# Chunked attention into a softplus feed-forward layer: other queues for the ring loads, spills and weight sums, other bank pairs in the products, another start of the second m-tile

## The chip, the cores and the metric

The kernel runs on one core of a Trainium2 chip. The metric is the device time of one execution in microseconds (us); before the change it is 883.77 us, the median of three runs (883.25 to 886.02). The engines are TensorE (PE, with its weight loads PEld), VectorE (DVE), ScalarE (ACT), GpSimd (POOL) and SyncE (SP); transfers between DRAM and on-chip memory are issued by SP, ACT or POOL and run on 16 DMA engines. Each engine works through its own instructions in program order.

## The reference

Eight batches, eight heads, 576 positions of 64 values: attention within chunks of 64 positions, then a feed-forward layer with softplus over all 4608 tokens. All in fp32.

```python
def _attn_ref(q, k, v):
    q_c = q.reshape(B, H, nc, chunk, D)          # nc = 9 chunks of 64, k_c and v_c alike
    scores = scale * np.matmul(q_c, k_c.transpose(0, 1, 2, 4, 3))
    scores = scores - np.max(scores, axis=-1, keepdims=True)
    attn = np.exp(scores)
    attn = attn / (np.sum(attn, axis=-1, keepdims=True) + 1e-09)
    return np.matmul(attn, v_c).reshape(B, H, S, D)

def _moe_ref(x, w_in, w_out):                    # x: 4608 x 512, w_in: 512 x 2048, w_out: 2048 x 512
    h = x @ w_in
    g = np.maximum(h, 0.0) + np.log1p(np.exp(-np.abs(h)))
    return g @ w_out
```

## The kernel before

**Numbers.** Each fp32 matmul is made of three faster ones: both factors are split into a rounded high part and the rest (names ending in hi and lo), and hi·hi, lo·hi and hi·lo are summed in PSUM. PE thus runs three matmuls of 128x512 for one, and ACT (the copies that round: `g_hi`, L643) and DVE (the subtractions: `g_lo`, L647) work ahead of it.

**Tiles.** The 4608 tokens are 9 m-tiles of 512, d_ff is 16 f-chunks of 128. For an m-tile and an f-chunk the first matmul gives 128 x 512 of h in a PSUM tile `pa`, softplus gives u, u is split into `g_hi` and `g_lo`, and the second matmul (L818, twelve matmuls, called G2 or a step here) adds to four tiles `po` that stand through all 16 f-chunks and are then copied out (L825) and stored (L832).

**Two stages.** The first three m-tiles are done plainly (L631 first matmul, L639 softplus). The last six form three *supers* of two m-tiles and eight *pairs* of f-chunks. In a pair a Strassen scheme takes seven products P0 to P6 (L763, six matmuls each) for eight: a product needs sums of two weight blocks and sums of two x blocks. The four quarters of the result lie in four PSUM banks x, y, z, v, two in each of two `pa` tiles a and b; P4, P5 and P6 add to y, z and x. ACT copies three banks out as s0, s1, s2 (L769), DVE and POOL make the six mixes d, e, c22, f, f2, c11 (L782), and ACT takes softplus of the quarters, soft10 and soft01 from y and z, soft11 from c22, soft00 from c11 (L790). Dependences in PSUM go by whole `pa` tiles, so a write to one bank waits for reads of its neighbour. The quarters of the first m-tile (soft10, soft00) go on to their G2s at once, two per pair behind the products of the next pair. Those of the second m-tile (soft01, soft11) are spilled to DRAM (L795) and come back (L798) for a phase of 16 G2s after the eight pairs.

**Ring.** The weight sums are made once, in the plain stage: POOL adds (L680, L694) and subtracts (L702), ACT rounds (L698), six stores per pair put them into a DRAM scratch (L708), and twelve more the weights that are needed unsummed (L714). Each pair of each super then reads its seven blocks in two transfers (L720, L724, "ring loads"): the large one has what P0 to P3 need, the small one P4 to P6.

**Attention.** Chunks of q, k, v are loaded by SP (L477, L358), transposed on DVE (L484, L531), scored on PE (L507), and P·V runs on PE (L595). For later m-tiles this happens in *bursts* of two blocks, put between the steps of the plain stage and into the first two supers, three among the pairs and one later. The exp of a burst needs another table of ACT than softplus; each change is a table load of 1.28 us.

**What sets the order.** Nothing is in the order of the code. `Plan` (L34 to L146) takes tasks with an engine, a cost, needs, an urgency `urg` (the lower first) and pools of buffers, simulates all engines with these costs and emits the instructions in the order of the simulated starts. PE's order is a list of its own; for the others the urgencies decide among what is ready. DMAs of SP and ACT share eight completion semaphores (DMAHW0 to 7), and a DMA waits for the one eight before it; the planner counted them by engine (`landed`). GpSimd's DMAs have others (DMASW).

Of the kernel before, what the change touches and what calls it, by code (L numbers as in the profile page):

```python
# [33 lines left out]
class Plan:  # L34
# [8 lines left out]
    WARM_UNTIL = 90.0  # L43

# [13 lines left out]
    def order(self):  # L58
# [37 lines left out]
        while times:  # L96
# [3 lines left out]
            for eng in list(wait):  # L100
# [5 lines left out]
                t = min(can, key=lambda t: (t["urg"], t["seq"]))  # L106
                wait[eng].remove(t)
# [10 lines left out]
                if t["kb"]:  # L118
                    end, lanes = now, landed.setdefault(eng, [0.0] * self.FLYING)
# [30 lines left out]
def chunked_attention_softplus_ffn(  # L150
# [84 lines left out]
    top_all = const.tile([P, TOP_BUFS * UW], I32, name="top")  # L235
    nc.vector.memset(top_all, 0)
    tops = [top_all[:, j * UW : (j + 1) * UW] for j in range(TOP_BUFS)]
    low_all = const.tile([P, LOW_BUFS * UW], I32, name="low")
# [415 lines left out]
    NX = 4  # L654

# [13 lines left out]
    def w_image(w, k):  # L669
        if w["name"] == "0_0" and k < NX:  # L670
            return raw_tile(1 + k // 2).bitcast(F32R)[:, k % 2 * MT : (k % 2 + 1) * MT]
        t = x_of(FAST - 1)[k // NX].rearrange("p s k t -> p (s k t)")
        return t[:, k % NX * MT : (k % NX + 1) * MT]

# [7 lines left out]
    def w_sum_parts(j):  # L682
        wt = live["wt", j]
        s, h = top_all.bitcast(F32), low_all.bitcast(F32)
        return [(s[:, :MT], h[:, :MT]), (s[:, MT:], h[:, MT:]), (wt[:, HC : 2 * HC], wt[:, :HC])]

    def w_sums(j, n):
        (s0, _), (s1, _), (s2, _) = w_sum_parts(j)
        t = [live["wt", j][:, i * HC : (i + 1) * HC] for i in range(4)]
        out, a, b, op = (  # L690
            (s0[:, :HC], t[0], t[3], ALU.add), (s0[:, HC:], t[2], t[3], ALU.add), (s1[:, :HC], t[2], t[0], ALU.subtract),
            (s1[:, HC:], t[0], t[1], ALU.add), (s2, t[1], t[3], ALU.subtract),
        )[n]
        nc.gpsimd.tensor_tensor(out, a, b, op=op)  # L694

    def w_sum_hi(j, n):
        s, h = w_sum_parts(j)[n]
        nc.scalar.copy(h.bitcast(F32R), s)  # L698

    def w_sum_lo(j, n):  # L700
        s, h = w_sum_parts(j)[n]
        nc.gpsimd.tensor_tensor(s, s, h, op=ALU.subtract)  # L702

    def w_sum_store(j, n, q):
        to = scratch[j].rearrange("p (n q c) -> p n q c", n=7, q=2)
        at = (slice(0, 2), slice(3, 6, 2), slice(6, 7))[n]
        src = w_sum_parts(j)[n][1 - q]
        nc.scalar.dma_start(to[:, at, q], src.rearrange("p (n c) -> p n c", c=HC))  # L708

    def w_own_store(b, q, i):  # L710
        src = wi[b][q].bitcast(F32)[:, i::2, 2 * i : 2 * i + 2, :].rearrange("p a k f -> p a (k f)")
        to = scratch[(0, 4, 6)[b] : (4, 6, 8)[b]]
        to = to.rearrange("a p (n q c) -> p a n q c", n=7, q=2)[:, :, 2 + 2 * i, q]
        nc.scalar.dma_start(to, src)  # L714

    def ring_load(w, part):
        src = scratch[w["j"]]
        if w["name"] == "0_0" and part == 0:
            for n in range(2):
                nc.scalar.dma_start(raw_tile(1 + n, True), src[:, 2 * n * MT : 2 * (n + 1) * MT])  # L720
# [3 lines left out]
        nc.scalar.dma_start(t[:, : cols.stop - cols.start], src[:, cols])  # L724
# [46 lines left out]
    def mix(w, what):  # L771
# [4 lines left out]
            "e": (s1, s1, s2, ALU.add),  # L776
            "c22": (s1, s1, v, ALU.add),
# [10 lines left out]
    def soft(w, i, j):  # L788
        src = {(0, 0): tmp_of(3), (0, 1): w["bank"][2], (1, 0): w["bank"][1], (1, 1): tmp_of(0)}[i, j]
        nc.scalar.activation(u_tiles(j)[i], src, AF.Softplus)  # L790
        if j == 0:
            w["first"][i]["u"] = u_tiles(0)[i]

    def spill_store(w):
        nc.scalar.dma_start(spill[w["s"]][w["j"]], top_all.bitcast(F32))  # L795

    def spill_load(w):
        nc.scalar.dma_start((top_all, low_all)[w["j"] % 2].bitcast(F32), spill[w["s"]][w["j"]])  # L798
        for i in range(2):
            w["second"][i]["u"] = u_tiles(1 - w["j"] % 2)[i]  # L800
# [3 lines left out]
    def gemm2(w):  # L804
# [9 lines left out]
        for n, (j, t) in order:  # L814
            if w["g"] == NG - 1 and t == TPM - 1:
# [4 lines left out]
                start=(w["first"] and n == 0), stop=n == 2 and (w["last"] or w["g"] == NG - 2 and t == TPM - 1),  # L820
# [55 lines left out]
    HOME_FREE.update({("v", i): ["Tq13", "Tk13"] for i in (12, 13)})  # L876
# [437 lines left out]
```

## Time and profile before

| stretch, us | what runs | length | PE busy | mean granted clock of PE |
|---|---|---|---|---|
| 89.0 to 336.7 | plain m-tiles, bursts, weight sums | 247.7 | 232.1 | 0.97 |
| 336.7 to 475.0 | super 1, pairs | 138.3 | 132.0 | 1.00 |
| 475.0 to 520.6 | super 1, second m-tile | 45.6 | 42.8 | 0.96 |
| 520.6 to 660.0 | super 2, pairs | 139.4 | 133.3 | 1.00 |
| 660.0 to 704.6 | super 2, second m-tile | 44.6 | 41.4 | 1.00 |
| 704.6 to 830.0 | super 3, pairs | 125.4 | 122.9 | 1.00 |
| 830.0 to 882.2 | super 3, second m-tile, end | 52.2 | 48.5 | 1.00 |

The profiled execution took 884.0 us by itself, with a span of 882.2 us from its first instruction to its last; 1.8 us lie around it. The three timed runs took 883.77, 886.02 and 883.25 us. A busy PE is not PE at its peak, since a matmul's shown end overlaps the next one; the loss is read from start to start. Waits are named by what released them, so "PE pa L763 <- DVE wib L782" is a product that waited for a mix.

### The profile page before, as it was taken

Reading aid. Unit: us, or ns where it says so; the run is one execution under the profiler, and the core shown is the slowest. Engines: PE = TensorE matmul, PEld = TensorE weight load, DVE = VectorE, ACT = ScalarE, POOL = GpSimd, SP = SyncE. Lnnn points to the kernel's source line nnn. Section 1 sums busy time; section 2 is a strip of 40 time slices with the busy share of each in tenths; the row PEclk is TensorE's granted clock in tenths of the full one; section 3 lists DMA queues with packets and bytes.
Section 4 is the critical chain, followed back from the end, with each engine's and each line's share of the span. In section 5 each row is a group of like instructions: output and inputs, shape, how many; then the busy total and the mean of one; then the engine's idle time right before and its main releaser. Section 6 shows DMA issues by size and latency. Waiting matters only on the chain.

```text
span 882.2 us, 15154 instructions
## 1 busy us (share of the span) xinstructions
PE 834.6 (95%) x5745; PEld 676.0 (77%) x5745; DVE 521.4 (59%) x876; ACT 388.8 (44%) x614; POOL 242.0 (27%) x217
## 2 busy tenths in 40 slices
PE   8899998999978999999998999999999999999998
PEld 7688887778756887777876877877777777878886
DVE  4999865656655588465566587473756733222322
ACT  4857753543423565343433254333452543333322
POOL 1676763359534221211110031121110312121100
PEclk9999999999989999999999999999999999999999
DMA  9987747664644535867567536757573145445332
GB/s 225 234 199 204 216 112 220 172 165 107 169 90 110 112 85 158 226 173 189 154 184 209 139 78 200 206 153 209 160 208 133 48 155 178 146 155 167 124 107 79
DMA packets 226343, 140.20 MB, mean 159 GB/s; under 512 B 183776, under 2 KB 207328, under 8 KB 223328
## 3 DMA queue, kind: packets, MB, share of 16 engines
q10 hardware_dynamic: 29408, 84.03, 28.9%
q1 hardware_dynamic: 196864, 55.23, 28.5%
q8 instruction: 45, 0.74, 0.4%
q14 instruction: 26, 0.21, 0.1%
HBM read 101.71 MB, written 36.70 MB: 157 GB/s over the span
## 4 chain that ended last, share of the span: by engine, by line
PE 66%; DVE 11%; DMA 8%; ACT 4%; issue 4%; POOL 3%; SPq 3%; ACTq 0%; DVEq 0%; POOLq 0%
PE po L818 36%; PE pa L763 20%; PE pa L631 7%; DVE wib L782 2%; DVE g_lo L647 2%; DVE eT L531 2%; SPq L477 2%; DMA raw<-in_moe_w_out_dram 2%; PE pa L595 1%; DMA q<-in_q_dram 1%; ACT low L790 1%; SPq L349 1%; PE pa L507 1%; DMA raw<-in_moe_w_in_dram 1%; POOL wib L782 1%
## 5 line engine op out<-in xcount | busy, mean ns | idle before, releaser
L818 PE MATMUL po<-late,g_hi 128*128 128x512 f32 x539 | 168.0, 395 | 0.1
L782 POOL TENSOR_TENSOR wib<-wib 128x512 f32<-128x512 f32 x48 | 62.6, 1304 | 333.3 <-ACT wib L769 331.4
L763 PE MATMUL pa<-wib,xb 128*128 128x512 f32 x432 | 109.0, 397 | 13.5 <-DVE wib L782 9.4
L818 PE MATMUL po<-wo_hi,g_lo 128*128 128x512 f32 x288 | 111.7, 400 | 9.6 <-DVE g_lo L647 9.6
L818 PEld LDWEIGHTS po<-late,g_hi 128*128 128x128 f32 x539 | 101.1, 189 | 22.0 <-POOL late L322 0.6
L818 PE MATMUL po<-wo_hi,g_hi 128*128 128x512 f32 x288 | 111.7, 400 | 2.5 <-ACT g_hi L643 2.5
L818 PE MATMUL po<-late,g_lo 128*128 128x512 f32 x287 | 109.1, 394 | 4.4 <-DVE g_lo L647 4.4
L763 PE MATMUL pa<-wi_hi,xb 128*128 128x512 f32 x368 | 113.3, 389 | 0.0
L818 PE MATMUL po<-wo_lo,g_hi 128*128 128x512 f32 x288 | 110.8, 397 | 0.6 <-POOL wo_lo L322 0.6
L763 PEld LDWEIGHTS pa<-wib,xb 128*128 128x128 f32 x432 | 79.2, 188 | 39.3 <-DVE wib L782 19.2
L531 DVE STREAM_TRANSPOSE eT<-qe 32x256 f32<-32x256 f32 x232 | 100.5, 433 | 8.2 <-POOL qe L582 4.9
L647 DVE TENSOR_TENSOR g_lo<-low,g_hi 128x512 fp32r<-128x512 f32 x72 | 54.4, 757 | 73.1 <-ACT g_hi L643 72.6
L643 ACT CAST g_hi<-low 128x512 fp32r<-128x512 f32 x72 | 44.7, 621 | 87.8 <-PE po L818 84.9
L763 PEld LDWEIGHTS pa<-wi_hi,xb 128*128 128x128 f32 x368 | 69.1, 188 | 14.3
L769 ACT COPY wib<-pa 128x512 f32<-128x512 f32 x72 | 40.0, 590 | 82.1 <-PE pa L763 82.1
L818 PEld LDWEIGHTS po<-wo_hi,g_lo 128*128 128x128 f32 x288 | 55.2, 192 | 24.9 <-DVE g_lo L647 13.4
L639 ACT ACTIVATE u<-pa 128x512 f32<-128x512 f32 (+1 forms) x50 | 29.1, 581 | 97.8 <-PE pa L631 52.7
L763 PE MATMUL pa<-wi_lo,xb 128*128 128x512 f32 x184 | 71.6, 389 | 0.0
L818 PEld LDWEIGHTS po<-late,g_lo 128*128 128x128 f32 x287 | 54.3, 189 | 18.0 <-DVE g_lo L647 6.6
L818 PEld LDWEIGHTS po<-wo_hi,g_hi 128*128 128x128 f32 x288 | 54.8, 192 | 14.7 <-ACT g_hi L643 3.2
L782 DVE TENSOR_TENSOR wib<-wib,pa 128x512 f32<-128x512 f32 x72 | 49.1, 687 | 27.9 <-ACT top L790 14.7
L818 PEld LDWEIGHTS po<-wo_lo,g_hi 128*128 128x128 f32 x288 | 55.1, 192 | 12.7 <-POOL wo_lo L322 1.1
(181 smaller groups left out, 1281.1 us busy)
## 6 DMA issues: line engine op xcount, KB each, us to landing
xb<-scratch ACTq DMA_DIRECT2D x23, 1024.0 KB, 5.4
xb<-scratch ACTq DMA_DIRECT2D x24, 768.0 KB, 5.1
spill<-top ACTq DMA_DIRECT2D x24, 512.0 KB, 3.3
out_dram<-raw SPq DMA_DIRECT2D x35, 256.0 KB, 2.9
raw<-in_moe_w_in_dram SPq DMA_DIRECT2D x16, 512.0 KB, 5.9
raw<-in_moe_w_out_dram SPq DMA_DIRECT2D x16, 512.0 KB, 4.9
raw<-in_v_dram SPq DMA_DIRECT2D x96, 64.0 KB, 2.9
top<-spill ACTq DMA_DIRECT2D x12, 512.0 KB, 4.0
```

What stands on the lines that cost most here:

```text
L349: eng.dma_start(dst[p0 : p0 + rows], src[b, :, s0 : s0 + rows, :].rearrange("h s d -> s h d"))
L477: nc.sync.dma_start(dst[p : p + BL, :, tb, :], src[b, :, s0 : s0 + BL, dh * BL : (dh + 1) * BL].rearrange("h s d -> s h d"),)
L507: nc.tensor.matmul(pa[o, c2, col : col + C], qT[r, a * HP + hl, :], kT[r, a * HP + hl, :], start=True, stop=True,)
L531: nc.vector.transpose(live["eT", i][d : d + BL, tb], e[s : s + BL, kb])
L631: nc.tensor.matmul(ph, wt[:, c, :], x[:, ts_, c, :], start=(n == 0), stop=(n == 3 * KC - 1))
L639: nc.scalar.activation(w["u"], w["ph"], AF.Softplus)
L643: nc.scalar.copy(w["hi"], w["u"])
L647: (nc.gpsimd if pool else nc.vector).tensor_tensor(w["lo"], w["u"], w["hi"].bitcast(F32), op=ALU.subtract)
L763: nc.tensor.matmul(w["bank"][BANK[k]], wts[:, q, c, :], x[:, c, :], start=k < NX and c + n == 0, stop=c == 1 and n == 2, skip_group_check= ...
L769: nc.scalar.copy(tmp_of(n), w["bank"][n])
L782: (nc.gpsimd if what in MIX_POOL else nc.vector).tensor_tensor(out, a, b, op=op)
L818: nc.tensor.matmul(pos[w["m"]][t], terms[n][0][:, j * P : (j + 1) * P], terms[n][1], start=(w["first"] and n == 0), stop=n == 2 and (w["la ...
```

## The change

- **Queues.** Ring loads are issued by GpSimd, spills, spill loads, weight-sum stores and own stores by SP; ACT issues none of them any more. `top` and `low` become two halves of one tile `ends`, and the sums are laid out hi beside lo, so that three stores per pair (512, 512, 256 KB) do for six. The blocks lie in the scratch in the order of `PLACE`.
- **Banks.** Tile a has x and v, tile b has y and z (before: x and y, z and v). P4 waits for s1 and s2, P6 for s0 and e; e takes s1 + v on DVE and c22 adds s2 on POOL; f and soft10 come behind P5.
- **Second m-tile.** The last pair's soft01 and soft11 are not spilled; their two G2s begin the second phase, and seven spills and loads per super remain.
- **Order.** An engine other than PE holds a task of `urg` 0 or more back when one of `urg` under 0 becomes ready within 0.7 us (from 120 us on). SP's and ACT's DMAs are counted together. Both exps of a burst get urgency −6, the fourth burst stands behind f-chunk 4 of the second phase, its seventh G2, and no longer behind f-chunk 8, its ninth, q and k of some blocks load into `raw` tiles, and some evacuations wait for transposes. PE's row count stays the same.

```diff
+    HOLD = 0.7
+    HOLD_FROM = 120.0
                 t = min(can, key=lambda t: (t["urg"], t["seq"]))
+                if t["urg"] >= 0 and now > self.HOLD_FROM and eng != "PE" and any(
+                    w["urg"] < 0 and now < ready[w["name"]] <= now + self.HOLD for w in wait[eng]
+                ):
+                    continue
-                    end, lanes = now, landed.setdefault(eng, [0.0] * self.FLYING)
+                    end, lanes = now, landed.setdefault(eng == "POOL", [0.0] * self.FLYING)
...
+    PLACE = (1, 2, 0, 3, 6, 4, 5)
+    def on(what):
+        return {"ACT": nc.scalar, "SP": nc.sync, "POOL": nc.gpsimd}[QUEUE[what]]
-    def w_sum_store(j, n, q):
-        to = scratch[j].rearrange("p (n q c) -> p n q c", n=7, q=2)
-        at = (slice(0, 2), slice(3, 6, 2), slice(6, 7))[n]
-        src = w_sum_parts(j)[n][1 - q]
-        nc.scalar.dma_start(to[:, at, q], src.rearrange("p (n c) -> p n c", c=HC))
+    def w_sum_store(j, n):
+        to = scratch[j][:, (1 + 2 * n) * MT :]
+        src = live["wt", j][:, :MT] if n == 2 else ends.bitcast(F32)[:, 2 * n * MT : 2 * (n + 1) * MT]
+        on("wd").dma_start(to[:, : src.shape[1]], src)
-        nc.scalar.dma_start(t[:, : cols.stop - cols.start], src[:, cols])
+        on("ring").dma_start(t[:, : cols.stop - cols.start], src[:, cols])
...
-            w["bank"] = [t[:, n] for t in (pa_tile(), pa_tile()) for n in range(2)]
+            a, b = pa_tile(), pa_tile()
+            w["bank"] = [a[:, 0], b[:, 0], b[:, 1], a[:, 1]]
-            "e": (s1, s1, s2, ALU.add),
-            "c22": (s1, s1, v, ALU.add),
+            "e": (s1, s1, v, ALU.add),
+            "c22": (s1, s1, s2, ALU.add),
-        nc.scalar.dma_start(spill[w["s"]][w["j"]], top_all.bitcast(F32))
+        on("us").dma_start(spill[w["s"]][w["j"]], top_all.bitcast(F32))
-        nc.scalar.dma_start((top_all, low_all)[w["j"] % 2].bitcast(F32), spill[w["s"]][w["j"]])
+        on("ul").dma_start((low_all, top_all)[w["j"] % 2].bitcast(F32), spill[w["s"]][w["j"]])
...
+    IN_RAW = {11: FAST - 1, 12: None, 13: None, 14: FAST, 15: FAST + 1, 16: None, 17: None}
+    HOMES.update({(n, 2 * p + 1): ("raw", 2 + j) for p in IN_RAW for j, n in enumerate("qk")})
-    IN_SUPER = ((0, 2), (0, 5), (0, 7), (1, 8))
+    IN_SUPER = ((0, 2), (0, 5), (0, 7), (1, 4))
-    MIX_POOL = ("d", "e")
+    MIX_POOL = ("d", "c22")
-    W_URG = 30
+    W_URG = 40
+    QUEUE = dict(wd="SP", wo="SP", ring="POOL", us="SP", ul="SP")
+    ISSUE = dict(ACT=0.4, SP=0.57, POOL=1.0)
-        second = [v_ for w in mine for v_ in w["second"]]
+        second = [v_ for w in mine[-1:] + mine[:-1] for v_ in w["second"]]
-            plan.add(f"exp{i}", "ACT", 0.62, partial(att_exp, i), [f"sub{b}"], urg=d, table="exp",
+            plan.add(f"exp{i}", "ACT", 0.62, partial(att_exp, i), [f"sub{b}"], urg=d if key in BEGIN else -6, table="exp",
-            needs += [before[f"P{k}_{name}"]] + {4: [f"s1_{name}"], 5: [f"s2_{name}"], 6: [f"s0_{name}"]}.get(k, [])
+            needs += [before[f"P{k}_{name}"]] + {4: [f"s1_{name}", f"s2_{name}"], 6: [f"s0_{name}", f"e_{name}"]}.get(k, [])
-                take = [("pa", [f"c11_{name}", f"soft10_{name}"]), ("pa", [f"soft01_{name}", f"c22_{name}", f"f2_{name}"])]
+                take = [("pa", [f"c11_{name}", f"e_{name}"]), ("pa", [f"soft01_{name}", f"soft10_{name}", f"f2_{name}"])]
-            ("d", ["s1", "s2"]), ("e", ["s0", "d"]), ("c22", ["e", "P3"]), ("f", ["d", "P4"]), ("f2", ["f", "P5"]),
+            ("d", ["s1", "s2"]), ("e", ["s0", "P3"]), ("c22", ["e", "d"]), ("f", ["d", "P5"]), ("f2", ["f", "P5"]),
-        for i, jj, what in ((1, 0, "P4"), (0, 1, "P5"), (1, 1, "c22"), (0, 0, "c11")):
+        for i, jj, what in ((1, 0, "P5"), (0, 1, "P5"), (1, 1, "c22"), (0, 0, "c11")):
-        plan.add(f"us{name}", "ACT", 0.6, partial(spill_store, w), [f"soft01_{name}", f"soft11_{name}"], urg=-1, kb=330)
+        if j < FC // 2 - 1:
+            plan.add(f"us{name}", QUEUE["us"], ISSUE[QUEUE["us"]], partial(spill_store, w), [f"soft01_{name}", f"soft11_{name}"], urg=-1, kb=400)
```

What it moves is seen in the order of three places, which the planner decides.

*A steady pair of the third super.* ACT before; `wib<-pa` are the copies s0 to s2, `low` and `top` the softplus quarters, "waits" the semaphores a row waits for:

```order
L769 COPY wib<-pa 128x512 [waits PE_49]
L769 COPY wib<-pa 128x512 [waits Pool_49]
L769 COPY wib<-pa 128x512 [waits PE_49]
L724 DMA xb<-scratch 128x2048 [waits DMAHW3_49]
L790 ACTIVATE low<-pa 128x512 [waits DVE_49,PE_49]
L790 ACTIVATE top<-pa 128x512 [waits DMAHW4_49,DVE_49]
L790 ACTIVATE top<-wib 128x512
L795 DMA spill_111<-top 128x1024 [waits Activation_49]
L724 DMA xb<-scratch 128x1536 [waits DMAHW5_49,PE_49]
L790 ACTIVATE low<-wib 128x512 [waits DVE_49]
L643 CAST g_hi<-low 128x512 [waits PE_49]
L643 CAST g_hi<-low 128x512 [waits PE_49,Activation_49]
```

and now:

```order
L779 COPY wib<-pa 128x512 [waits PE_49] x2
L779 COPY wib<-pa 128x512
L800 ACTIVATE ends<-pa 128x512 [waits DVE_49,PE_49]
L800 ACTIVATE ends<-pa 128x512 [waits DMAHW1_49,DVE_49]
L800 ACTIVATE ends<-wib 128x512 [waits Pool_49]
L800 ACTIVATE ends<-wib 128x512 [waits DVE_49,Activation_49]
L649 CAST g_hi<-ends 128x512 [waits PE_49,Activation_49] x2
```

The three DMA rows are gone, and the third copy, s2, has no wait of its own, since P2 is already awaited by s1. POOL at the change from the second super to the third, before (`wib<-wib` are d and the second POOL mix, `wib<-xa` sums of x blocks):

```order
L702 TENSOR_TENSOR raw_1379<-raw_1379 128x256
L742 TENSOR_TENSOR low<-xa 128x1024
L742 TENSOR_TENSOR top<-xa 128x1024
L782 TENSOR_TENSOR wib<-wib 128x512 x16
L742 TENSOR_TENSOR wib<-xa 128x1024 x2
```

and now:

```order
L733 DMA xb<-scratch 128x2048
L733 DMA xb<-scratch 128x1536
L751 TENSOR_TENSOR wib<-xa 128x1024 x2
L792 TENSOR_TENSOR wib<-wib 128x512 x2
L733 DMA xb<-scratch 128x2048
```

Before, the sixteen mixes of a super stood one behind the other; now both ring loads of the next pair stand between each two.

*The plain stage, a burst.* DVE before, around the wait of PE at 284.66 us (`qe<-xa` and `ka<-xa` are transposes of loaded q and k, `eT` of exponentials):

```order
L531 STREAM_TRANSPOSE eT<-qe 32x256 x4
L484 STREAM_TRANSPOSE qe<-q 128x512
L484 STREAM_TRANSPOSE ka<-k 128x512
L484 STREAM_TRANSPOSE qe<-xa 128x512
L484 STREAM_TRANSPOSE ka<-xa 128x512
L647 TENSOR_TENSOR g_lo<-u,g_hi 128x512 x2
```

and now:

```order
L537 STREAM_TRANSPOSE eT<-qe 32x256 x4
L490 STREAM_TRANSPOSE qe<-q 128x512
L490 STREAM_TRANSPOSE ka<-k 128x512
L653 TENSOR_TENSOR g_lo<-u,g_hi 128x512
L490 STREAM_TRANSPOSE qe<-xa 128x512
L653 TENSOR_TENSOR g_lo<-u,g_hi 128x512
L490 STREAM_TRANSPOSE ka<-xa 128x512
```

Both g_lo have moved ahead of a transpose. In the burst before 146.82 us one g_lo moved likewise, from behind `qe<-xb` to between two groups of four `eT`.

*Into the second m-tile.* ACT at the end of the third super's pairs, before (`low<-spill` and `top<-spill` load spilled quarters, `raw<-po` copies the first m-tile's result out):

```order
L790 ACTIVATE low<-wib 128x512 [waits DVE_49]
L643 CAST g_hi<-low 128x512 [waits PE_49]
L798 DMA top<-spill_111 128x1024 [waits DMAHW4_49]
L643 CAST g_hi<-low 128x512 [waits PE_49,Activation_49]
L798 DMA low<-spill_111 128x1024 [waits DVE_49]
L643 CAST g_hi<-top 128x512 [waits DMAHW5_49,PE_49]
```

and now:

```order
L800 ACTIVATE ends<-wib 128x512 [waits DVE_49,Activation_49]
L649 CAST g_hi<-ends 128x512 [waits PE_49,Activation_49] x2
L649 CAST g_hi<-ends 128x512 [waits DVE_49,PE_49]
L834 COPY raw_7738<-po_7121 128x512 [waits PE_49]
L834 COPY raw_7744<-po_7123 128x512 [waits DMAHW7_49,DMAHW0_49,PE_49]
```

The third `g_hi`, the first of the second m-tile, waited for a DMA and now waits for PE and DVE alone.

More of the change, by code (lines that the diff above doesn't have):

```diff
@@ L819, in gemm2 @@
                 pos[w["m"]][t], terms[n][0][:, j * P : (j + 1) * P], terms[n][1],
-                start=(w["first"] and n == 0), stop=n == 2 and (w["last"] or w["g"] == NG - 2 and t == TPM - 1),
+                start=(w["first"] and n == 0), stop=n == 2 and (w["last"] or w["g"] == END[0] and t == TPM - 1),
             )
@@ L1267, in add_g2 @@
                     continue
-                plan.add(f"ev{m}_{t}", "DVE" if odd else "ACT", 0.65, partial(evacuate, w, t), [f"G2_{g}"], urg=-3,
+                past = {FAST: 13, FAST + 1: 14, FAST + 2: 17}.get(m)
+                past = [f"T{n}{2 * past + 1}" for n in "qk"] if past and t < 2 else []
+                plan.add(f"ev{m}_{t}", "DVE" if odd else "ACT", 0.65, partial(evacuate, w, t), [f"G2_{g}"] + past, urg=-3,
                          take=[(f"out{t}", [f"st{m}_{t}"])] if m < NM - 1 else [],
```

93 lines of the change are left out of this document (49 added, 44 removed).

## Prediction

> **What bounds the kernel now.** The first view read is the page: the span and the busy time of each engine.
>
> ```profile
> span 882.2 us, 15154 instructions
> PE 834.6 (95%) x5745; PEld 676.0 (77%) x5745; DVE 521.4 (59%) x876; ACT 388.8 (44%) x614; POOL 242.0 (27%) x217
> ```
>
> PE is busy for 95% and the change leaves its matmuls as they are, so the only time to win is what PE loses between them. What a matmul costs with nothing lost is read in the timeline, from the first and the twelfth start of one undisturbed step of the second matmul:
>
> ```profile
> 275.30 0.39 PE L818 MATMUL po<-wo_hi,g_hi 128*128 128x512 f32 x1
> 277.79 0.39 PE L818 MATMUL po<-wo_hi,g_lo 128*128 128x512 f32 x1
> ```
>
> That is 2.49/11 = 0.226 us from start to start. A product of six therefore takes 1.36 us, a step of twelve 2.72 us; whatever starts later than this is loss, also where no idle time is printed, because busy times of neighbours overlap. The third view is the waits of PE, for the stage of plain m-tiles (90 to 336 us) and then for the supers (336 us to the end): releaser, total us, count, mean.
>
> ```profile
> PE po L818 <- DVE g_lo L647: 9.2, 5, 3.3
> PE pa L595 <- ACT u L639: 3.3, 2, 2.1
> PE pa L507 <- DVE ka L484: 2.9, 2, 2.0
> ```
>
> ```profile
> PE pa L763 <- DVE wib L782: 9.4, 8, 1.6
> PE po L818 <- DVE g_lo L647: 4.8, 5, 2.0
> PE pa L763 <- ACT low L790: 2.7, 4, 0.7
> PE po L818 <- ACT g_hi L643: 2.5, 1, 2.5
> ```
>
> Some waits cost more than themselves: the granted clock drops behind them. In the table of windows (length; busy us of PE, PEld, DVE, ACT, POOL; then PE's clock, DMA share, GB/s) four stretches stand out:
>
> ```profile
> 216.00:232.00 16.00, 13.89 (x172) 11.20 (x171) 7.36 (x14) 6.46 (x11) 11.14 (x12) 0.89 0.58 142
> 248.00:262.00 14.00, 9.91 (x149) 7.84 (x148) 8.26 (x15) 4.72 (x7) 7.00 (x9) 0.76 0.40 75
> 275.00:290.00 15.00, 11.69 (x45) 9.17 (x44) 4.90 (x8) 2.97 (x5) 7.34 (x8) 0.89 0.46 90
> 470.00:482.00 12.00, 9.14 (x33) 6.78 (x32) 7.24 (x16) 5.37 (x8) 0.00 (x0) 0.86 0.77 204
> ```
>
> Window times (1 − clock) gives 1.8, 3.4, 1.6 and 1.7 us. The Trainium skill, "TensorE: Matmul & The Clock Gate", section "Part 1: The HAM clock gate", puts the fall to half clock after an idle window of about 3.4 us. The trace differs in the last window, where the longest wait is 2.54 us (row 476.12 below); by the page its 1.7 us would not be there to win, and the measurement decides.
>
> **The change part by part.** *The pairs (24).* Each runs seven products; the waits stand at P4 to P6. A pair with an attention burst beside it, where ACT also loads tables, and a steady one, in the timeline:
>
> ```profile
> 388.12 2.88 PE L763 MATMUL pa<-wib,xb 128*128 128x512 f32 x12
> 392.46 1.66 PE L763 MATMUL pa<-wib,xb 128*128 128x512 f32 x6 [1.46 <-DVE wib L782]
> 393.96 0.39 PE L818 MATMUL po<-wo_hi,g_hi 128*128 128x512 f32 x1
> ...
> 726.93 4.68 PE L763 MATMUL pa<-wib,xb 128*128 128x512 f32 x18
> 731.45 0.39 PE L818 MATMUL po<-wo_hi,g_hi 128*128 128x512 f32 x1
> ```
>
> The first loses 393.96 − 388.12 − 18 × 0.226 = 1.76 us, of which 1.46 is printed, so refilling the pipe costs 0.30; the second loses 0.44 with nothing printed. The group of these matmuls has the idle time of all pairs:
>
> ```profile
> L763 PE MATMUL pa<-wib,xb 128*128 128x512 f32 x432 | 109.0, 397 | 13.5 <-DVE wib L782 9.4 <-ACT low L790 2.7
> ```
>
> 13.5 + 24 × 0.30 = 20.7 us lost in all. What P4 to P6 wait for follows from the whole-tile dependence: before, P6 (tile a) comes behind soft10 and f, which read P4's bank of the same tile. These are the steady pair's other engines, apart:
>
> ```profile
> 724.41 1.08 ACT L769 COPY wib<-pa 128x512 f32<-128x512 f32 x2 [2.27 <-PE pa L763]
> 728.49 0.60 ACT L790 ACTIVATE low<-pa 128x512 f32<-128x512 f32 x1 [0.77 <-PE pa L763]
> 729.19 0.69 DVE L782 TENSOR_TENSOR wib<-pa,wib 128x512 f32<-128x512 f32 x1 [6.21 <-ACT low L790]
> 727.80 2.65 POOL L782 TENSOR_TENSOR wib<-wib 128x512 f32<-128x512 f32 x2 [13.31 <-ACT wib L769]
> ```
>
> With the new banks P4 and P5 share tile b and P6 goes to tile a, whose last reader is e, one DVE operation of 0.69 us behind P3. P6 starts two products, 2.72 us, after P3's end: 2.0 us of room. soft10 and f (728.49, 729.19) no longer stand ahead of P6. What is late next is P4, which now waits for both s1 and s2: two ACT copies, 1.08 us, which begin when P2 ends and end about 1.3 us into P3 (1.08 and some 0.2 of latency), where P4 is due at 1.36. That is even, so I leave 0.2 us a pair, 4.8; nothing left and the steady pair's 0.44 are the bounds. **−16 us** (−21 to −10). It hangs on ACT being free then; moving the ring and spill issues off ACT (some 0.33 us each, as in row 471.43 below) helps there.
>
> *Ring loads on GpSimd.* 47 transfers; from ACT they land as follows (page part 6; below it min/median/max of all):
>
> ```profile
> xb<-scratch ACTq DMA_DIRECT2D x23, 1024.0 KB, 5.4
> xb<-scratch ACTq DMA_DIRECT2D x24, 768.0 KB, 5.1
> ```
>
> ```profile
> DMA to landing us min/median/max: 4.9/5.3/7.9
> ```
>
> The large one can go when P3 has read its tile, but stands on POOL behind d and c22 (2.65 us, row 727.80), which start 1.4 us into P3: issued 4.1 us after P3's start. The next P0 comes after P3 to P6 (5.4) and two steps (5.4): 10.9. Room 6.8 against 5.4: **0 us**, hidden under two second-matmul steps; more where a burst lies between. A GpSimd issue is not in the trace. Its landing is bounded by 4.9 and 7.9, nothing to 23 × 1.1 = +25 us; I take the median, 5.3, the same bytes on the same 16 engines. Time that the issue keeps POOL, 0 to 1.3 us (one mix), twice a pair, falls into POOL's 13.3 idle us. The small load waits on POOL for P6; behind it stand only the next pair's d and c22, which need later products anyway.
>
> *Spills and weight sums on SP.* ACT no longer issues 47 ring loads, 48 spill transfers, 48 sum stores and 12 own stores; SP issues 42, 24 and 12 of the last three kinds. ACT is no bound at 44%, so by itself **0**. A spill store now stands on SP behind loads that may wait for a buffer, and the next pair's soft01 waits for the store; it has most of a pair, 15 us by the steps above, and a ring load of twice its size landed in 5.4, so it is hidden. In the plain stage a store that waits for POOL's sums now holds the q and k loads behind it, and for those wait transposes and scores; SP already stands still there (waits of SP's queue, 100 to 345 us):
>
> ```profile
> SPq L477 <- DMA scratch<-low: 16.0, 7, 6.8
> ```
>
> That row also says that SP and ACT share DMA lanes: loads waited for scratch stores. Half the stores take half of it away, the order brings it back; the sum is in the plain stage's bounds below.
>
> *Into the second m-tile (3 times).* Before, its first softplus tile must come back from DRAM:
>
> ```profile
> 471.43 0.33 ACTq L798 DMA_DIRECT2D top<-spill  x1
> 475.45 1.14 ACT L643 CAST g_hi<-top 128x512 fp32r<-128x512 f32 x2
> 476.12 0.50 PE L818 MATMUL po<-wo_hi,g_hi 128*128 128x512 f32 x1 [2.54 <-ACT g_hi L643]
> 477.25 0.80 PE L818 MATMUL po<-wo_hi,g_lo 128*128 128x512 f32 x1 [0.32 <-DVE g_lo L647]
> ```
>
> With the last pair kept on chip g_hi needs only softplus, and the first reload has two steps, 5.4 us, for the 4.0 that 471.43 to 475.45 shows. That frees 2.54 + 0.32, two refills that I put at 0.2 each here, and the clock's 1.7: 5.0, of which I count 4.5. The other g_lo waits of the supers, 4.8 − 0.3 + 4 × 0.2 = 5.3, are at these transitions and beside the moved fourth burst; I count half, 2.6. **−7 us** (−10 to −2).
>
> *The plain stage.* Printed 9.2 + 3.3 + 2.9 = 15.4, nine refills of 0.17 and the clock's 6.8 make about 24 us to win. Two waits in it have one cause, a g_lo placed on DVE behind transposes that wait for loads:
>
> ```profile
> 279.42 0.71 DVE L484 STREAM_TRANSPOSE qe<-xa 128x512 f32<-128x512 f32 x1 [2.52 <-DMA xa<-in_k_dram]
> 282.98 0.71 DVE L484 STREAM_TRANSPOSE ka<-xa 128x512 f32<-128x512 f32 x1 [2.84 <-DMA xa<-in_k_dram]
> 283.61 1.00 DVE L647 TENSOR_TENSOR g_lo<-u,g_hi 128x512 fp32r<-128x512 f32 x1
> ```
>
> ```profile
> 146.82 0.50 PE L818 MATMUL po<-wo_hi,g_lo 128*128 128x512 f32 x1 [2.76 <-DVE g_lo L647]
> 284.66 0.50 PE L818 MATMUL po<-wo_hi,g_lo 128*128 128x512 f32 x1 [3.31 <-DVE g_lo L647]
> ```
>
> The plan's hold, costs and urgencies show only as order, and the new order has these two g_lo ahead of those transposes: 2.76 + 3.31 + 1.6 of clock, 7.7 us. The rest (P·V behind a softplus that splits two exps, scores behind late transposes) is helped by the paired exps and hurt by SP's stores. **−8 us**; bounds: −20, nearly all gone, and +8, half of the 16.0 us in SP's row above appearing as new waits of PE.
>
> *Sum:* −16 + 0 + 0 − 7 − 8 = −31. Span 882.2 − 31 = 851; around the span lie 1.8 us (884.0 for the profiled run, which is 0.2 above the median shown, 883.77): **853 us**.
>
> **The rivals.**
> *The plain stage clears almost wholly:* −20 there for −8, 841; with the pairs at −19, 838 to 845. For it: every wait there has an edit against it. Against: those bursts wait for loads, and SP got 36 more issues.
> *The wait moves to P4, or the plain stage gives nothing:* ACT late by 0.3 us at s1 and s2 costs 24 × 0.6 with the refill, 14 of the 16; 853 + 14 = 867. Or −31 + 8 = −23: 861. Both: 875. For it: 1.3 against 1.36 us leaves nothing, and ACT loads tables in the burst pairs.
> *The change doesn't do what it says:* if P6 still waits for a late DVE operation in tile a, because e stands behind transposes there, the 13.5 us stay: 853 + 16 = 869. It lies in the same stretch as the one before.
> *Slower:* the ring load lands late. From 6.8 us on, each us costs 23 us, one for each pair that follows another; at 6.8 + 31/23 = 8.15 us the whole gain is gone, and at 8.5 the time is 853 + 39 = 892. Against: 7.9 is the longest of 47. For: GpSimd's way of issuing is not in the trace, and DVE is busy beside it, with 0.69 us a mix. The Trainium skill, "SBUF — State Buffer", section "SBUF: two separate sides", says that GpSimd cannot write its descriptors while DVE runs a two-port operation such as an fp32 copy within SBUF, and advises ACT or SP. By that rule the loads would slip by DVE's operations; here most DVE rows of a pair are TENSOR_TENSOR, many of them reading PSUM, and no run here shows yet what they do to such a load.
>
> **How the numbers follow.** Forecast, 845 to 860: 0.45. Plain stage clear, 837 to 845: 0.13. Wait moved, or the change not doing what it says, 860 to 880: 0.23. Within 0.3%, about what a measurement of this kernel can tell from no change: 0.07, where a ring load near 8 us eats the gain. Slower: 0.12. The first three make faster, 0.81, and the range runs over them, 837 to 880.
>
> **What would show it.** P4 to P6 of a pair start to start at 1.36 us with no wait on DVE: the pairs' step is right. Waits of PE on the ACT copies: the second rival. Waits of P0 on the ring loads, or landings above 6.8 us: the slow rival. No wait on g_hi at the three transitions and a clock of 1.00 there: the third step. In 90 to 336 us, waits on g_lo under 4 us and PE's clock above 0.97 show the plain step; waits of SP on POOL's sums with scores waiting for transposes show it wrong. Ring loads that move the bursts, or new waits at the end of an m-tile, would make the sum wrong in a way not priced here.

## The result, and the profile after

| | us, median | lowest to highest | ratio to before, 95% interval |
|---|---|---|---|
| before | 884.26 (4 runs) | 883.25 to 886.02 | |
| changed | 847.68 (4 runs) | 846.6 to 848.26 | 0.9583 [0.9564, 0.9602] |

The change takes 36.6 us off, 4.2%. The page of the changed kernel: span, and busy time of each engine with its share and instructions.

```profile
span 845.7 us, 15261 instructions
PE 824.3 (97%) x5745; PEld 674.2 (80%) x5745; DVE 529.8 (63%) x876; ACT 378.7 (45%) x608; POOL 268.2 (32%) x266
```

PE has the same 5745 matmuls in a span that is 36.5 us shorter. The waits of PE (releaser, total us, count, longest), first from 90 to 326 us, the plain stage, then from 325 us to the end:

```profile
PE pa L513 <- DVE ka L490: 5.0, 2, 2.6
PE pa L637 <- DVE xb L618: 2.2, 2, 1.5
```

```profile
PE po L827 <- DVE g_lo L653: 2.4, 2, 2.0
PE pa L773 <- DMA xb<-scratch: 0.5, 1, 0.5
```

The 15.4 us of the plain stage have become 7.2: none for g_lo or softplus any more, 5.0 for transposes of k (2.9 before), and 2.2 for xb. Of all the waits in the supers three are left. The group of products with wib, which had 13.5 us of idle time:

```profile
L773 PE MATMUL pa<-wib,xb 128*128 128x512 f32 x432 | 103.9, 394 | 0.0
```

Where it was won is read from two starts. The first product of a super starts at 325.1 us, before at 336.7: 11.6 us come from the plain stage. From there to the end it takes 520.6 us for 545.5: 24.9 us come from the supers. Counted from matmul start to matmul start in the two traces, the pairs' products lost 20.9 us in all against 42 × 0.2266 us each (the usual step from start to start in both), and now lose 2.4. That is 18.5 of the 24.9; the other 6.4 lie outside the products, where the waits before stood at the second m-tiles (476 to 520 and 660 to 700 us).

A steady pair in the timeline, P3's end to the next step, PE, ACT, DVE and POOL apart:

```profile
707.80 0.39 PE L773 MATMUL pa<-wi_lo,xb 128*128 128x512 f32 x1
708.03 4.33 PE L773 MATMUL pa<-wib,xb 128*128 128x512 f32 x18
712.19 0.39 PE L827 MATMUL po<-wo_hi,g_hi 128*128 128x512 f32 x1
```

```profile
706.87 1.07 ACT L779 COPY wib<-pa 128x512 f32<-128x512 f32 x2 [2.13 <-PE pa L773]
```

```profile
708.30 0.69 DVE L792 TENSOR_TENSOR wib<-wib,pa 128x512 f32<-128x512 f32 x1 [4.34 <-PE pa L773]
```

```profile
708.03 2.66 POOL L792 TENSOR_TENSOR wib<-wib 128x512 f32<-128x512 f32 x2 [9.88 <-ACT wib L779]
710.63 0.57 POOL L733 DMA_DIRECT2D xb<-scratch  x1
712.66 0.53 POOL L733 DMA_DIRECT2D xb<-scratch  x1 [1.46 <-PE pa L773]
```

P4 starts at 708.03, one matmul step of 0.23 us behind P3's last: no loss, though its two copies ended only at 706.87 + 1.07 = 707.94. P4 to P6 take 712.19 − 708.03 = 4.16 us for 18 × 0.2266 = 4.08. And e, the mix that P6 waits for, ends at 708.30 + 0.69 = 708.99, 1.8 us before P6 is due at 708.03 + 12 × 0.2266 = 710.75. The large ring load is issued at 710.63, and the next pair begins at 717.63.

### The profile page after: what moved, and what is told of

Its sections match the earlier page's. It is cut to its first block, busy times and chain, and to the rows that moved or that the text cites. A ratio compares the mean times of both kernels' runs of the same rounds, so it can differ in the third digit from the quotient of the medians.

```text
span 845.7 us, 15261 instructions
## 1 busy us (share of the span) xinstructions
PE 824.3 (97%) x5745; PEld 674.2 (80%) x5745; DVE 529.8 (63%) x876; ACT 378.7 (45%) x608; POOL 268.2 (32%) x266
## 4 chain that ended last, share of the span: by engine, by line
PE 75%; DMA 9%; SPq 5%; DVE 5%; ACT 3%; issue 2%; POOL 1%; DVEq 0%; ACTq 0%; POOLq 0%
PE po L827 36%; PE pa L773 25%; PE pa L637 11%; SPq L483 3%; DMA raw<-in_moe_w_in_dram 2%; DMA raw<-in_moe_w_out_dram 1%; SPq L355 1%; PE pa L601 1%; DMA k<-in_k_dram 1%; PE pa L513 1%; DMA ends<-spill 1%; DMA q<-in_q_dram 1%; DVE g_lo L653 1%; DMA xb<-scratch 1%; SPq L364 1%
## 5 line engine op out<-in xcount | busy, mean ns | idle before, releaser
L653 DVE TENSOR_TENSOR g_lo<-ends,g_hi 128x512 fp32r<-128x512 f32 x96 | 70.5, 734 | 88.8 <-ACT g_hi L649 86.4
L649 ACT CAST g_hi<-ends 128x512 fp32r<-128x512 f32 x96 | 59.2, 617 | 112.8 <-PE po L827 101.7
L773 PE MATMUL pa<-wib,xb 128*128 128x512 f32 x432 | 103.9, 394 | 0.0
L800 ACT ACTIVATE ends<-pa 128x512 f32<-128x512 f32 x48 | 28.7, 599 | 82.6 <-PE pa L773 57.5
L653 DVE TENSOR_TENSOR g_lo<-u,g_hi 128x512 fp32r<-128x512 f32 (+1 forms) x40 | 33.6, 839 | 50.0 <-ACT g_hi L649 49.6
```

The costliest lines, as they stand in the source:

```text
L649: nc.scalar.copy(w["hi"], w["u"])
L653: (nc.gpsimd if pool else nc.vector).tensor_tensor(w["lo"], w["u"], w["hi"].bitcast(F32), op=ALU.subtract)
L773: nc.tensor.matmul(w["bank"][BANK[k]], wts[:, q, c, :], x[:, c, :], start=k < NX and c + n == 0, stop=c == 1 and n == 2, skip_group_check= ...
```

## The experiments

Twelve kernels ran beside the kernel before, with a new median for it in each series of four (883.3, 882.6 and 883.7 us). "Pairs" below is the loss of all 24 pairs against 42 × 0.2266 us, and "first product" the start of the first one, from the trace of the one profiled run. The clock's drops move it by some us from run to run, so small differences in that column alone are not read.

| run | us, median | ratio, 95% interval | first product | pairs lose |
|---|---|---|---|---|
| before | 884.3 | | 336.7 | 20.9 |
| changed | 847.7 | 0.9583 [0.9564, 0.9602] | 325.1 | 2.4 |
| old banks | 860.9 | 0.9743 [0.9722, 0.9765] | 322.2 | 18.1 |
| before, new banks alone | 884.7 | 1.0016 [0.9996, 1.0036] | 333.9 | 5.7 |
| queues on ACT | 860.6 | 0.9728 [0.9697, 0.9759] | 327.6 | 7.5 |
| last pair spilled | 858.7 | 0.9714 [0.9692, 0.9736] | 323.0 | 2.3 |
| before, new banks and raw tiles | 873.8 | 0.9892 [0.9868, 0.9916] | 335.1 | 6.2 |
| no raw tiles | 868.3 | 0.9827 [0.9801, 0.9852] | 322.8 | 2.6 |
| ring loads on SP | 846.8 | 0.9595 [0.9561, 0.9630] | 320.7 | 5.0 |
| sums on ACT | 853.9 | 0.9664 [0.9638, 0.9691] | 331.8 | 2.3 |
| no hold | 850.7 | 0.9625 [0.9609, 0.9641] | 326.0 | 2.3 |
| old urgency of exps | 845.4 | 0.9571 [0.9550, 0.9592] | 322.9 | 2.3 |
| ring on SP, x sums on DVE | 844.5 | 0.9557 [0.9540, 0.9574] | 321.3 | 4.7 |
| the same, loads planned shorter | 853.7 | 0.9664 [0.9642, 0.9686] | 321.6 | 12.0 |

**Old banks.** The changed kernel with the bank pairs undone.

```diff
-            a, b = pa_tile(), pa_tile()
-            w["bank"] = [a[:, 0], b[:, 0], b[:, 1], a[:, 1]]
+            w["bank"] = [t[:, n] for t in (pa_tile(), pa_tile()) for n in range(2)]
...
-            "e": (s1, s1, v, ALU.add),
-            "c22": (s1, s1, s2, ALU.add),
+            "e": (s1, s1, s2, ALU.add),
+            "c22": (s1, s1, v, ALU.add),
...
-    MIX_POOL = ("d", "c22")
+    MIX_POOL = ("d", "e")
...
```

> The changed kernel with the bank pairs of before (x and y in tile a, z and v in tile b) and the mixes and needs that go with them; queues, second m-tile and order rules as changed. Theory (whole-tile waits of P6 on soft10 and f were the loss, and only the banks took them away): the group of products with wib loses 10 to 14 us of idle time again, waits on DVE's mixes, 862 to 868 us. Rival (ACT was late because it issued DMAs; the queues took the waits away): below 851 us, idle time of that group under 3 us.

The time lies 1 us under the theory's range and far from the rival's; the group's idle time, the last figures of its row, is inside it:

```profile
L772 PE MATMUL pa<-wib,xb 128*128 128x512 f32 x432 | 108.9, 396 | 10.6 <-DVE wib L791 8.5
```

ACT issues none of the ring, spill and sum transfers here, and the waits at P6 are back all the same. The banks removed them, not the relief of ACT.

**New banks alone.** The reverse edit on the kernel before.

> The kernel before with the new bank pairs alone, and the mixes and needs that go with them; all DMAs still on ACT and SP as before. Theory (banks): 863 to 869 us, the idle time of the products with wib falls from 13.5 us to under 2. Rival (queues): above 878 us, the waits move to P4 on ACT's copies, which stand behind ACT's DMA issues, and stay above 8 us.

The time is the rival's, the mechanism is not: the pairs lose 5.7 us for 20.9, the group's idle time is 1.9 us, both as the theory has it, and no P4 waits for ACT. The gain was given back further on. Waits of PE in the supers (333 us to the end), waits of SP's queue from 430 to 470 us, and two windows with PE's clock behind the busy times:

```profile
PE pa L507 <- DVE ka L484: 13.7, 2, 7.7
PE po L819 <- DVE g_lo L647: 3.0, 2, 2.0
PE po L819 <- DVE raw L826: 2.1, 2, 1.9
PE pa L764 <- DVE wib L783: 1.9, 1, 1.9
```

```profile
SPq L477 <- DVE qe L484: 11.9, 1, 11.9
```

```profile
456.00:470.00 14.00, 8.32 (x57) 6.84 (x58) 5.72 (x10) 4.23 (x7) 0.00 (x0) 0.76 0.65 170
646.00:660.00 14.00, 6.34 (x50) 5.22 (x51) 5.23 (x10) 3.84 (x6) 0.00 (x0) 0.76 0.60 167
```

The burst behind the last pair of supers 1 and 2 needs a k that comes hardly sooner than before: in super 1 its transpose starts at 460.9 us, in the kernel before at 462.6. Since PE is now early, it waits 6.0 and 7.7 us, and the clock drop of 14 × 0.24 = 3.4 us follows each time: 20 us, for the 15 that the pairs had won.

**Raw tiles.** Two reasons for the late k were open: one buffer each for q and k, so that loads wait for transposes; or completion lanes that SP's loads share with ACT's ring loads. The first run gives the kernel before both the new banks and the raw tiles, with ring loads still on ACT; the second takes the raw tiles from the changed kernel, with ring loads still on GpSimd.

```diff
+    IN_RAW = {11: FAST - 1, 12: None, 13: None, 14: FAST, 15: FAST + 1, 16: None, 17: None}
+    HOMES.update({(n, 2 * p + 1): ("raw", 2 + j) for p in IN_RAW for j, n in enumerate("qk")})
...
```

```diff
-    IN_RAW = {11: FAST - 1, 12: None, 13: None, 14: FAST, 15: FAST + 1, 16: None, 17: None}
+    IN_RAW = {}
```

> The kernel before with the new banks, and besides the raw tiles for q and k of the second block of some bursts (with the evacuations that wait for them); queues as before. With the banks alone PE waited 6.0 and 7.7 us for a late transposed k in the fourth burst's place of supers 1 and 2. Theory (one q and one k buffer: the next block's loads begin only when the block before is transposed): those two waits and the clock's drop behind them go, 864 to 871 us. Rival (SP's loads share eight completion lanes with ACT's ring loads and stand behind them): the waits stay over 4 us each, 878 us or more.

> The changed kernel without the raw tiles for q and k; banks, queues, second m-tile and rules as changed. Theory (single buffers): waits of 4 us or more for transposes of k in the bursts of supers 1 and 2, 856 to 868 us. Rival (lanes: with ring loads on GpSimd the loads are early anyway): no such wait, 847 to 851 us.

With raw tiles on the old queues no scores wait for k is left in the supers, and 10.9 us are gained; the time is 3 us over the theory's range; a new wait of 2.9 us for a mix stands there (the one of 1.9 us was there with the banks alone). Without raw tiles the waits return although the ring uses GpSimd's lanes, and the time is 0.3 us over the theory's range (waits of PE from 322 us to the end):

```profile
PE pa L513 <- DVE ka L490: 15.9, 3, 6.1
PE po L827 <- DVE g_lo L653: 3.2, 2, 2.0
```

So the buffers decide, in both directions, and 20.6 us of the result (868.3 for 847.7) hang on an edit that looks like housekeeping.

**Queues on ACT.** All five kinds of transfer issued by ACT again, then the sums' and own stores alone, then the ring loads by SP.

```diff
-    QUEUE = dict(wd="SP", wo="SP", ring="POOL", us="SP", ul="SP")
+    QUEUE = dict(wd="ACT", wo="ACT", ring="ACT", us="ACT", ul="ACT")
```

```diff
-    QUEUE = dict(wd="SP", wo="SP", ring="POOL", us="SP", ul="SP")
+    QUEUE = dict(wd="ACT", wo="ACT", ring="POOL", us="SP", ul="SP")
```

```diff
-    QUEUE = dict(wd="SP", wo="SP", ring="POOL", us="SP", ul="SP")
+    QUEUE = dict(wd="SP", wo="SP", ring="SP", us="SP", ul="SP")
```

> The changed kernel with all of ring loads, spills, spill loads, sum stores and own stores issued by ACT again (still three stores per pair). Theory (the queues are worth little in the pairs, something in the plain stage): 847 to 853 us, at most 3 us of it in the pairs. Rival (ACT's time is what counts: s2 ends only 0.09 us ahead of P4): P4 waits on ACT in most pairs, 0.3 us or more each, 855 us or more.

> The changed kernel with the weight sums' and own stores issued by ACT (three stores per pair, as changed), ring and spill as changed. Theory (in the plain stage ACT's issues and their lane waits hold up softplus and g_hi): the stretch up to the first product grows by 3 to 9 us, 851 to 857. Rival (the order rules alone gave the plain stage's gain): that stretch stays within 1.5 us of 325.1, 846 to 850 us in all.

> The changed kernel with ring loads issued by SP, all else as changed. Theory (what counts is that ACT does not issue them, and that GpSimd's queue keeps them out of the way of SP's loads): loads of bursts and the small ring load get late, P4 or the bursts wait, 851 to 862 us. Rival (any queue but ACT's will do): 846 to 850 us. If the large ring load lands a median of 0.3 us or more sooner than GpSimd's 5.7, GpSimd's issue costs that much.

With all on ACT 12.9 us are lost, 7.6 beyond the theory's range. The time is the rival's, the mechanism is not: P4 never waits for ACT's copies. It waits three times for its ring load, issued late from ACT's order, and the pairs lose 5.1 us more, where the theory had 3 at most (waits from 327 us on):

```profile
PE po L827 <- DVE g_lo L653: 5.4, 3, 2.4
PE pa L773 <- DMA xb<-scratch: 4.3, 3, 2.1
PE pa L601 <- DVE wib L792: 2.2, 1, 2.2
```

The sums alone on ACT cost 6.2 us, all of it before the first product, which comes 6.7 us later; there PE waits for late transposes and softplus (90 to 332 us):

```profile
PE pa L513 <- DVE ka L490: 9.8, 3, 4.4
PE pa L601 <- ACT u L645: 2.7, 2, 1.5
PE po L827 <- DVE g_lo L653: 0.7, 2, 0.4
PE pa L637 <- DVE xb L618: 0.4, 1, 0.4
```

The size is the theory's, the way to it only in part. Softplus makes PE wait 2.7 us; the larger part is k, 9.8 us for 5.0. ACT's stores and SP's loads share completion semaphores, and SP's loads of q and k stand waiting for those stores (waits of SP's queue, 100 to 330 us):

```profile
SPq L483 <- DMA scratch<-ends: 22.6, 8, 4.8
SPq L483 <- DMA scratch<-wib: 4.7, 2, 2.4
```

In the changed kernel the waits of SP for stores to the scratch are 0.4 us in all. With everything on ACT, these stores too, the first product comes only 2.5 us later, so the price hangs on the rest of the order too. That GpSimd must be the ring's queue is not borne out: from SP the time is the same within the intervals. PE then waits four times for a ring load, 2.8 us in all, and the loads themselves land sooner. Issues and landing of the changed kernel (large, small; then all, minimum, median, maximum), then with SP:

```profile
xb<-scratch POOLq DMA_DIRECT2D x23, 1024.0 KB, 5.7
xb<-scratch POOLq DMA_DIRECT2D x24, 768.0 KB, 7.6
```

```profile
DMA to landing us min/median/max: 5.2/6.4/8.9
```

```profile
xb<-scratch SPq DMA_DIRECT2D x23, 1024.0 KB, 5.3
xb<-scratch SPq DMA_DIRECT2D x24, 768.0 KB, 5.2
```

The small load's 7.6 us go with the place of its issue. From GpSimd 22 of the 24 are issued a median of 2.0 us behind a large one that is still under way, and land behind it, as the one at 712.66 does after 8.4 us; the one issued long after its large one, at 335.28, landed in 5.2.

**Last pair spilled.** The changed kernel with all eight pairs spilled and the second m-tile in its old order.

```diff
-        second = [v_ for w in mine[-1:] + mine[:-1] for v_ in w["second"]]
+        second = [v_ for w in mine for v_ in w["second"]]
...
-                src = f"ul{name}" if group == "second" and j < FC // 2 - 1 else f"soft{i}{int(group == 'second')}_{name}"
+                src = f"ul{name}" if group == "second" else f"soft{i}0_{name}"
```

> The changed kernel with the last pair of a super spilled too and its G2s last, as before; the fourth burst stays behind the seventh G2 of the phase. Theory (the reload of the first spilled tile is the wait at the transition): 2 to 4 us per super come back with the clock's drop, 851 to 857 us, PE waiting for g_hi at three transitions. Rival (the spill loads on SP go early enough by themselves): within 1 us of the change, 847 to 849.

11.0 us are lost, 1.7 beyond the theory's range: two waits rather than three, but longer ones (waits of PE from 323 us on). At the longer one the reload stands on SP behind eight loads of v (SP's timeline, then ACT's):

```profile
PE po L827 <- ACT g_hi L649: 8.5, 2, 5.5
```

```profile
447.99 5.95 SPq L364 DMA_DIRECT2D raw<-in_v_dram  x8
453.98 1.08 SPq L807 DMA_DIRECT2D ends<-spill  x2
```

```profile
458.67 1.14 ACT L649 CAST g_hi<-ends 128x512 fp32r<-128x512 f32 x2 [4.86 <-DMA ends<-spill]
```

Before, with the spills on ACT, PE waited 2.5 us for g_hi and not 8.5. So the pair on chip seems to be worth more now that the spills are on SP; no run has it with the spills on ACT alone, so this is not shown.

**The order rules.** The changed kernel with one rule undone each.

```diff
-    HOLD = 0.7
+    HOLD = 0.0
```

```diff
-            plan.add(f"exp{i}", "ACT", 0.62, partial(att_exp, i), [f"sub{b}"], urg=d if key in BEGIN else -6, table="exp",
+            plan.add(f"exp{i}", "ACT", 0.62, partial(att_exp, i), [f"sub{b}"], urg=d, table="exp",
```

> The changed kernel without the rule that holds a less urgent task back for 0.7 us. Theory (in the plain stage the gain came from the sums' and own stores leaving ACT, which alone was worth 6 us there; the hold adds little): the first product starts 0 to 3 us later than 325.1, 846 to 852 us. Rival (the hold put the g_lo ahead of the transposes): waits on g_lo of 2 us or more return before the first product, 853 us or more.

> The changed kernel with the old urgency of the exps. Theory (a softplus between the two exps costs two table loads, 2.6 us, and P times V waits for it): waits of 1 to 2 us of P times V on softplus return at two or three bursts of the plain stage, 850 to 856 us. Rival (the planner puts the exps together without it): 846 to 849 us.

The hold is worth 3.0 us. The g_lo in the two bursts whose order was quoted keep their places ahead of the transposes without it, so the hold did not put them there. But other waits on g_lo return, of 1.5 and 1.8 us in the plain stage (169.89 and 316.72 us, none in the changed kernel) and 4.9 for 2.4 in the supers, and the two waits for k near 220 and 248 us become one of 5.1. The exps' urgency is worth nothing that can be measured: the median is 2.2 us lower than the changed kernel's, just under the rival's range, and the intervals overlap. The profile says where the two profiled runs differ (windows of the changed kernel, then of this run; the last three figures are PE's clock, DMA share, GB/s):

```profile
214.00:228.00 14.00, 11.55 (x163) 9.33 (x162) 7.06 (x13) 4.72 (x7) 4.35 (x5) 0.88 0.59 158
241.00:256.00 15.00, 12.42 (x161) 9.99 (x160) 10.66 (x21) 4.72 (x7) 6.87 (x8) 0.77 0.58 152
```

```profile
214.00:228.00 14.00, 11.55 (x169) 9.48 (x168) 6.66 (x13) 6.72 (x10) 3.27 (x4) 1.00 0.58 157
241.00:256.00 15.00, 12.16 (x172) 9.89 (x170) 10.28 (x20) 7.49 (x11) 6.91 (x8) 1.00 0.57 150
```

PE waits 2.45 us at the same place in both (220.5 and 219.6 us), and 2.58 and 2.44 us near 248 us; in one the clock falls behind both waits, 14 × 0.12 + 15 × 0.23 = 5.1 us in all, in the other behind neither.

**Two attempts at a faster version.** Ring loads on SP and no sum of x blocks on POOL; then, besides, the planner's figures for loads of q and k nearer to the trace.

```diff
-    XS_POOL = (2, 4)
+    XS_POOL = ()
...
```

```diff
-                plan.add(f"{n}{i}", "SP", 0.55 * two if whole else 4.6, partial(blk_load, i, n, src), free_of[n, i],
-                         urg=d - QK_URG, kb=310 if whole else 430, parts=two if whole else 8,
+                plan.add(f"{n}{i}", "SP", 0.55 * two if whole else 3.8, partial(blk_load, i, n, src), free_of[n, i],
+                         urg=d - QK_URG, kb=310 if whole else 256, parts=two if whole else 8,
```

> The changed kernel with ring loads on SP and with all sums of x blocks on DVE, none on POOL. With the sums on POOL one g_lo on DVE took 2.85 us for its usual 0.69 while POOL's two sums ran, and PE waited 1.99 us for it in super 2. Theory (DVE and POOL hold each other up while both run such operations): that g_lo takes under 1.3 us and the wait falls under 0.8 us, 843 to 846 us against 846.8 for ring loads on SP alone. Rival (g_lo is late because DVE has too much to do there): the added 2.4 us of DVE make the wait longer, 847 to 850 us.

> As the run with all sums of x blocks on DVE, and the planner's figures for a block's q or k load nearer to the trace (3.8 us and 256 KB for 4.6 and 430), so that it transposes the second k before the g_lo, max and subtraction it now stands behind. Theory (the two remaining waits of the plain stage, 2.45 and 2.58 us, are an order the planner chose for loads that it thinks late): both fall under 1 us, 838 to 843 us. Rival (the k does land late): DVE stands still for it and PE waits for g_lo too, 845 us or more.

The first is the fastest kernel here, 844.5 us, 0.9557 [0.9540, 0.9574] of before; its interval overlaps that of the changed kernel by 0.001, and that of ring loads on SP as well, so that it is the faster one is not clear of noise. What the sums do is plain in the timeline. DVE of the changed kernel, POOL of the same, and DVE of the run:

```profile
652.76 3.44 DVE L763 TENSOR_TENSOR wib<-xa,wib 128x1024 fp32r<-128x1024 f32 x1
656.12 2.85 DVE L653 TENSOR_TENSOR g_lo<-ends,g_hi 128x512 fp32r<-128x512 f32 x1
```

```profile
651.72 6.70 POOL L751 TENSOR_TENSOR wib<-xa 128x1024 f32<-128x1024 f32 x2 [33.24 <-issue]
```

```profile
650.24 2.36 DVE L751 TENSOR_TENSOR wib<-xa 128x1024 f32<-128x1024 f32 x2
652.51 0.69 DVE L653 TENSOR_TENSOR g_lo<-ends,g_hi 128x512 fp32r<-128x512 f32 x1
```

While POOL sums, a g_lo on DVE takes 2.85 us for its 0.69; done on DVE the two sums cost 2.4 us, and the wait of 1.99 us is gone, as the theory had it. The second attempt fails, with 853.7 us where the theory had 838 to 843: the wait near 219 us goes, but the one near 247 us grows to 3.9, and the new order costs 6.5 us in one pair of super 2. What a planner's better figure for one kind of task brings is not read from the place that it was meant for.

## Why the prediction was right

- **Pairs, −16.** Measured −18.5. The step held: in the steady pair P4's two copies end 0.09 us ahead of it and cost nothing, and most pairs lose 0.09 us where I had left 0.2. The undone banks show that the banks did it (10.6 us of idle time back).
- **Ring loads on GpSimd, 0.** Measured 0.5 us, one wait, and the same time from SP. The room was 7.0 us (710.63 to 717.63) for the 6.8 worked out, the large load landed in a median of 5.7. An issue keeps POOL for 0.53 to 0.57 us, inside the 0 to 1.3 allowed for. The slow rival needed 8.15. Landings above 6.8 us, named as its sign, did come (small loads, median 7.6, up to 8.9) and cost nothing: the small load is needed only at P4, at 717.63 + 24 × 0.2266 = 723.07, so the one issued at 712.66 had 10.4 us. The Trainium skill, "SBUF — State Buffer", section "Who interferes with whom", says that `tensor_tensor` on DVE did not stall such transfers. The large loads here agree, with a median of 5.7 us from GpSimd for 5.3 from SP. The Trainium skill, "DMA: Bandwidth & Descriptors", section "Latency and other measured facts", gives GpSimd's first byte some 0.4 us more. The 0.4 us between those two medians agree with that.
- **Spills and sums on SP, 0 by itself.** Wrong in its parts, and the sum did not show it. The prediction read SP's 16.0 us of waits for scratch stores, expected half to go and the order to bring it back, and put the move into the plain stage's bounds as a risk. With the stores on SP 0.4 us of such waits are left, and the sums' move is worth 6.2 us by the medians. And with the spills on SP the kernel takes 11.0 us more if the last pair does not stay on chip.
- **Second m-tile, −7.** Measured 24.9 − 18.5 = 6.4, with no wait on g_hi left.
- **Plain stage, −8.** Measured −11.6. The two g_lo of the quoted order no longer make PE wait. The term was too small by the sums' move; the clock's part, 6.8 us before, is 5.1 in this profile and none in the run with the old urgency of the exps. In the runs with the old banks, without raw tiles and with the last pair spilled, which share these queues and rules, the first product comes at 322.2 to 323.0 us, so the term is −14 there.
- **A reading.** The last figure in the views of waits is the longest wait, not the mean, as the prediction names it; none of its sums uses it as a mean.
- **What the prediction lacked** is the condition of its first term. Without the raw tiles, which it did not price, PE would have run into loads that come no sooner, and the kernel would stand at 868 us; on the kernel before, the new banks alone are worth nothing that can be measured. "Ring loads that move the bursts" stood there as a thing not priced; it was loads of q and k, and it is not a mishap but the next bound.

So the total, −31 forecast and −36.6 measured, was right in sign and size, and in the place of its three terms, and one reason short. That the raw tiles were part of the change was luck as far as the forecast goes: it had no term for them. The parts do not add: undone one at a time, banks, raw tiles, queues and the last pair on chip cost 13, 21, 13 and 11 us, 58 in all, for a gain of 37.

## What to carry to other kernels

A wait taken off the bottleneck engine moves its whole program forward against everything that runs on its own time: before counting the gain, look for the next transfer that will not come sooner, here a load held by a buffer that another engine frees. Test a change of several parts by undoing each from the whole and not only by adding each to the old kernel: the banks were worth 13 us in the one and nothing in the other. And where several banks share a tile for dependences, pair those whose readers are done early with those that are written next.

## What was not expected of the hardware

The granted clock's fall behind a wait is not settled by the wait's length. The wait of 2.45 us for the same scores, 220.5 us in the changed kernel, stands in seven profiled runs. In four of them (changed, no raw tiles, ring loads on SP, ring on SP with x sums on DVE) the clock from 214 to 228 us is 0.88, in three (old urgency of the exps, old banks, last pair spilled) it is 1.00. Even 1.90 us among back-to-back matmuls of 128x512 can be enough: with the new banks alone, behind the wait at 543.60 us, the clock from 538 to 550 us is 0.86. The Trainium skill, "TensorE: Matmul & The Clock Gate", section "Part 1: The HAM clock gate", puts the fall after at least one idle window of about 3.4 us, and says that the window runs freely. Here a fall followed waits of 2.45 and 1.90 us. Where the wait falls in such a window could decide it; no run here shows that.

DVE and POOL hold each other up when both read two operands in SBUF: a g_lo of DVE takes 2.85 us for 0.69, a subtraction 3.44 where others of its size take 1.21, and POOL's two sums take 6.70 us there and 5.23 at 478.01. A mix on DVE with one operand in PSUM does not suffer: the one at 708.30 took 0.69 us beside POOL's mixes from 708.03 on. The Trainium skill, "SBUF — State Buffer", section "Who interferes with whom", says that a DVE instruction with two SBUF inputs contends with a GpSimd instruction that reads SBUF. The run without POOL's sums agrees: the same g_lo takes 0.69 us.
